# The opening of a Nyström-attention and two-layer kernel, emitted from a written list of single steps

## The chip, the cores and the metric

The kernel runs on one core of one Trainium2 chip. The metric is device time in microseconds (us) from the start to the end of the program on that core. The engines named below are PE (matmuls), DVE (vector), ACT (activations and copies), POOL (GpSimd), and SP, which here only issues DMA transfers. Each engine takes its instructions strictly in the order in which the program emits them, so the order of emission decides what an engine waits for.

## What is computed

A batch of 8 with 8 heads of 576 rows and 64 columns goes through a Nyström approximation of attention with 32 landmarks, and the result through two feed-forward blocks. Cut to what matters:

```python
q_lm, k_lm = mean of q and of k over each of 32 segments of 18 rows
A, Bm, C = softmax(q k_lm'), softmax(q_lm k_lm'), softmax(q_lm k')   # all scaled by 1/8
Z = Bm' / (norm1(Bm) * norminf(Bm) + 1e-6)
for _ in range(6): Z = 2 * Z - Z @ Bm @ Z
x = A @ Z @ C @ v                        # 4608 tokens, 512 wide
h = ((x @ w1) * (x @ w2)) @ w3           # 1024 wide, the gated block
x = h @ w_out1
g = elu(x @ w_in2)                       # 2048 wide
out = g @ w_out2
```

## The kernel before

**Stages.** The program has an opening, then 128 gated units, then 72 units of the second block. A gated unit is one batch, one half of its 576 rows and one eighth of the 1024 columns of the gated block. `ab(u)` makes its two products on PE (12 matmuls into two PSUM buffers), `ab_product(u)` copies one of them on ACT and multiplies on DVE, `ab_split(u)` splits the product into a high and a low part (ACT, then DVE), and `yy(u)` multiplies both with the folded weight and accumulates over eight units (12 matmuls).

**What the opening has to make.** (1) The weights arrive as 64-bit words and are rebuilt as float32, in 40 *conversions* of 128x512 in the opening (16 of w3, 8 of w_out1, 16 of w1 and w2 together). One conversion is: a load by SP, two ACT instructions (tiles `w_y` or `wo_y`, and `w_r` or `wo_r`), a short 16-bit DVE instruction on `w_y` or `wo_y`, a longer one into `cw` or `sw`, and an addition, on POOL for all but two conversions. Each of two pools has three buffers for what is loaded, so a load waits until an older conversion has been read. (2) w3 and w_out1 are folded into one weight by 16 *fold steps* on PE of four 128x512 matmuls (`w3o_step`, tile `w3acc`, 8 matmul records each in the trace). (3) The attention of batch 0, and most of that of batch 1: sums of q and k on DVE, scores `b`, `c` and `a` on PE, six Newton steps `n`, each a PE product and a DVE update of X, the transposes `ct`, the products `cv` and `z`, and the tiles `m` (`m_tiles`, one of four column groups each: eight matmuls, two copies `mh` on ACT, two differences `ml` on DVE). Unit 0 needs z, two `m` tiles and the rows `ath`/`atl` of `a`.

**Buffers that couple the steps.** All small attention products (`b`, `c`, `a`, `n`, `ct`, `cv`, `z`, `m`) share two PSUM buffers (`ps_at`, `bufs=2`): the next such product waits until ACT or DVE has read the one two before it. The pair of products of `ab` has two more (`ps_mm`).

**What sets the order.** Conversions are generators in `Pipe`, two at a time in the order of `ORDER`: each tick of the loop moves every running pair on by one stage and starts one new pair. After each tick the loop runs 1 or 2 half steps (`RATE = 1.6`) of the attention of batch 0, from the table that `Attention.steps` fills, and the half steps at which batch 1 is loaded and summed are given by `L1S`, `KS` and `QS`:

```python
while (i - A0) * RATE < NST or (1, NP - 1) not in w12_done or w3o_left:
    pipe.tick(len(pipe.todo) > n_late - HOLD)
    ...
    for hs in range(int((i - A0) * RATE), int((i - A0 + 1) * RATE)):
        run_steps(st0, hs)
```

Within a tick the four stages of a pair stand together on each engine: both `w_y`, both `w_r`, both long DVE instructions, both additions. The first two `m` tiles follow the loop. Then units start at u = 0 in the loop over `units`, whose `fill` runs half steps of the next batches, the last conversions of w1 and w2, and the conversions of the second block's weights (`pipe2`).

Of the kernel before, what the change touches and what calls it, by code (L numbers as in the profile page):

```python
# [24 lines left out]
NP = H // 2  # L25
# [22 lines left out]
QS = 20  # L48
RATE = 1.6
GAP = 2  # L50
CONV = (1, 5, 11, 14, 18)
M2 = 5
M3 = 10
VT = 7
W3B = 5
AH = 1
LT = 1
H_MAX = 4079.0


@with_exitstack
def nystrom_moe_kernel(ctx, tc, qT, kT, vm, vr, w12, w3T, w_out1, w_in2, w_out2, out):
# [60 lines left out]
    def high_parts(jobs):  # L123
# [3 lines left out]
        for c in jobs:  # L127
# [5 lines left out]
    def bits_job(jobs, ahead=2, late=1):  # L133

        for c in jobs:
            load_raw(c)
        for _ in range(ahead):  # L140
            yield
        for c in jobs:
            c.y, c.r = c.t("y", "cy", BF16), c.t("r", "ct", U32)
            act.activation(c.y, c.top.bitcast(BF16), AF.Abs, scale=2.0 ** -112)
        for c in jobs:
            act.mul(c.r, c.mid, 2.0 ** -13)
        high_parts(jobs)
        yield
        for c in jobs:
            if callable(c.x):  # L150
                c.x = c.x()
            (dve if c.on_dve else pool).tensor_tensor(c.x.bitcast(U32), c.b, c.r, op=ALU.add)
        for _ in range(late):
            yield
        for c in jobs:
            if c.done is not None:
                c.done()

    held, spills = set(), []

# [125 lines left out]
    def flush():  # L286
        while later:
            later.pop(0)()
# [334 lines left out]
    stp = start_ctx.enter_context(tc.tile_pool(name="start", bufs=1))  # L623

    with tc.manual_schedule():
        pipe = Pipe()
        wo_x, w3_x, acc = {}, {}, {}
        w3o_out = []
        w3o_left = {(ph, k) for ph in range(2) for k in range(K1)}

        def run_steps(st, i):
            for f, a in st.get(i, ()):
# [2 lines left out]
        def w3o_step(ph, k):  # L635
            if k == 0:
                acc[ph] = [ps_acc.tile([128, 512], F32, name=f"w3acc{ph}{j}", tag=f"acc{j}") for j in range(4)]
            for j in range(4):
                pe.matmul(acc[ph][j], w3_x[ph, k][:, j * 128 : (j + 1) * 128], wo_x[k], start=(k == 0), stop=(k == K1 - 1))
            w3o_left.remove((ph, k))  # L640
            if k == K1 - 1:
                for j in range(4):
                    o = (w3o_hi[4 * ph + j], w3o_lo[4 * ph + j], acc[ph][j])
                    if ph == 0:
                        split(*o)
                    else:
                        w3o_out.append(o)

        def wo_tile(k):
            wo_x[k] = stp.tile([128, DM], F32, name=f"wo{k}")  # L650
# [6 lines left out]
        w12_done = set()  # L657

        def w12_conv(p, jn, hp, on_dve):
            return Conv(  # L660
                p, f"w12{jn}{hp}", w12[hp, :, jn * 512 : (jn + 1) * 512], on_dve,
                x=w12_sb[:, hp, jn * 512 : (jn + 1) * 512], done=lambda: w12_done.add((jn, hp)),
            )

        def w3_conv(p, ph, k, on_dve):
            return Conv(
                p, f"w3{ph}{k}", w3T[k * 128 : (k + 1) * 128, ph * 512 : (ph + 1) * 512], on_dve,
                x=lambda: w3_tile(ph, k), done=lambda: w3o_step(ph, k),
            )

        w12_todo = [(jn, hp) for jn in range(4) for hp in range(NP)]
        w3_todo = [(ph, k) for ph in range(2) for k in range(K1)]

        def w12_next(p, on_dve):
            return w12_conv(p, *w12_todo.pop(0), on_dve)

        def w3_next(p, on_dve):
            return w3_conv(p, *w3_todo.pop(0), on_dve)

        n_wo = 0  # L680
        for o in ORDER:
            if o == "A":
                k, n_wo = n_wo, n_wo + 1
                wo = Conv(cvp, f"wo{k}", w_out1[k * 128 : (k + 1) * 128, :], False, x=lambda k=k: wo_tile(k))
                pair = [wo, w3_next(stp, k < E2)]
            elif o == "P":
                pair = [w3_next(cvp, False), w3_next(stp, False)]
            elif o == "B":
                pair = [w12_next(cvp, False), w3_next(stp, False)]
            elif o == "W":  # L690
                pair = [w12_next(cvp, False), w12_next(stp, False)]
            pipe.add(bits_job(pair, ahead=AH, late=LT))
        n_late = len(w12_todo)
        while w12_todo:
            pipe.add(bits_job([w12_next(cvp, False)]))

        make_words(cvp, "cw")
        make_words(stp, "sw")
        for w in PRE:
            if w != "-":  # L700
                load_in(0, w)
            pipe.tick()
        make_identity(nc, ident)
        for bd in (*qpad, cvbd):
            pool.memset(bd, 0.0)
# [6 lines left out]
        for hp in range(NP):  # L712
            st0[hp].extend(st0.pop((-16, -14, -12, -11)[hp]))
        L1 = dict(zip("kqv", L1S))
        S1 = {}
        for hp in range(NP):
            for w, o, hs in (("k", KS, (-16, -14, -12, -11)[hp]), ("q", QS, hp)):
                steps[1].pop(hs)
                S1.setdefault(o + hp, []).append((w, hp))
        i = 0  # L720
        while (i - A0) * RATE < NST or (1, NP - 1) not in w12_done or w3o_left:
            pipe.tick(len(pipe.todo) > n_late - HOLD)
            if i == VT:
                load_in(0, "v")
            for hs in range(int((i - A0) * RATE), int((i - A0 + 1) * RATE)):
                run_steps(st0, hs)
                for w in "kqv":
                    if hs == L1[w]:
                        load_in(1, w)
                for w, hp in S1.pop(hs, ()):  # L730
                    atts[1].sums(w, hp)
            i += 1
        for n, rest in enumerate(S1.values()):
            steps[1].setdefault(n, []).extend((atts[1].sums, wh) for wh in rest)
        start_ctx.close()
        mlp_ctx = ExitStack()
        mlp = mlp_ctx.enter_context(tc.tile_pool(name="mlp", bufs=1))

        units = [(b, n, fc) for b in range(B) for n in range(2) for fc in range(K1)]
        gt = {}  # L740
# [201 lines left out]
        def fill(b, hs):  # L942
            run_steps(steps[b + 1], hs)
            run_steps(steps[b], hs + 32)
            run_steps(steps[b + 2], hs - 32)
            if pipe.busy():
                pipe.tick()
            else:
                pipe2.tick(hs in CONV)
            if w3o_out:  # L950
                split(*w3o_out.pop(0))
            mt = [(atts[b + 1], m_next[hs])] if b + 1 < B and hs in m_next else []
            own = m_own if b else m_first
            if hs in own:
                while (own[hs], NP - 1) not in w12_done:
                    pipe.tick()
                mt.append((atts[b], own[hs]))
# [130 lines left out]
```

## Time and profile before

| | us |
|---|---|
| median of 3 runs | 1403.71 (1403.01 to 1405.25) |
| the profiled execution | 1403.01 |
| its span, first to last instruction | 1401.2 |
| first matmul of unit 0 | 105.1 |
| first matmul of unit 16 | 178.3 |
| PE busy, whole span | 1356.7 (97%) |

The page splits the span into 40 slices of 35 us. From the fifth slice on PE is busy at 9 tenths or more in each but the last; in the first four it stands at 6, 8, 7 and 8 tenths. The granted clock of PE reads 9 tenths or more in every slice but the third, where it reads 8. So the stretch to read is the first 180 us, by engine and by wait. A busy PE there includes matmul records stretched by a wait for their operands.

### The profile page before, as it was taken

Reading aid. Unit: us, or ns where it says so; the run is one execution under the profiler, and the core shown is the slowest. Engines: PE = TensorE matmul, PEld = TensorE weight load, DVE = VectorE, ACT = ScalarE, POOL = GpSimd, SP = SyncE. Lnnn points to the kernel's source line nnn. Section 1 sums busy time; section 2 is a strip of 40 time slices with the busy share of each in tenths; the row PEclk is TensorE's granted clock in tenths of the full one; section 3 lists DMA queues with packets and bytes.
Section 4 is the critical chain, followed back from the end, with each engine's and each line's share of the span. In section 5 each row is a group of like instructions: output and inputs, shape, how many; then the busy total and the mean of one; then the engine's idle time right before and its main releaser. Section 6 shows DMA issues by size and latency. Waiting matters only on the chain.

```text
span 1401.2 us, 26871 instructions
## 1 busy us (share of the span) xinstructions
PE 1356.7 (97%) x10848; PEld 1175.1 (84%) x10848; DVE 1031.0 (74%) x1830; ACT 628.3 (45%) x1263; POOL 332.5 (24%) x351
## 2 busy tenths in 40 slices
PE   6878999999999999999999999999999999999998
PEld 2326888988898889898899899899899899899897
DVE  6887867686668675635887878788687787878774
ACT  5535453545344444433353444344344453444342
POOL 5541425334345345112201011010100101011000
PEclk9989999999999999999999999999999999999999
DMA  9853454554474453246965564655655555564540
GB/s 339 276 175 129 153 174 155 200 191 135 158 260 142 157 183 128 101 157 254 367 221 189 208 220 159 229 199 188 207 196 214 176 223 189 206 223 158 196 150 31
DMA packets 59468, 266.76 MB, mean 190 GB/s; under 512 B 5584, under 2 KB 14800, under 8 KB 47056
## 3 DMA queue, kind: packets, MB, share of 16 engines
q0 software_dynamic: 12672, 140.51, 27.8%
q1 hardware_dynamic: 46672, 124.54, 25.6%
q8 instruction: 85, 1.39, 0.4%
q14 instruction: 39, 0.32, 0.1%
HBM read 223.08 MB, written 41.94 MB: 189 GB/s over the span
## 4 chain that ended last, share of the span: by engine, by line
PE 72%; DVE 2%; DMA 1%; ACT 0%; issue 0%; SPq 0%; ACTq 0%; DVEq 0%
PE o L919 9%; PE o L918 9%; PE o L917 9%; PE hm L858 9%; PE hm L859 8%; PE hm L860 8%; PE y L780 3%; PE ab L753 3%; PE y L782 2%; PE y L781 2%; PE ab L754 2%; PE ab L755 2%; PE m L331 1%; DMA w_raw<-in_w_in_dram 1%; PE n L615 0%; PE cv L387 0%
## 5 line engine op out<-in xcount | busy, mean ns | idle before, releaser
L858 PE MATMUL hm<-yb,wh 128*128 128x256 f32 x1008 | 285.2, 283 | 2.5 <-DVE g L876 1.7
L859 PE MATMUL hm<-yb,wh 128*128 128x256 f32 x1008 | 285.0, 283 | 0.0
L860 PE MATMUL hm<-yb,wh 128*128 128x256 f32 x1008 | 284.9, 283 | 0.0
L919 PE MATMUL o<-wo,el 128*128 128x512 f32 x576 | 225.6, 392 | 0.0
L918 PE MATMUL o<-wo,eh 128*128 128x512 f32 x576 | 225.3, 391 | 0.0
L917 PE MATMUL o<-wo,eh 128*128 128x512 f32 x576 | 224.0, 389 | 0.0
L889 ACT ACTIVATE t<-m 128x512 f32<-128x512 f32 x144 | 89.9, 624 | 297.9 <-DVE m L887 297.9
L858 PEld LDWEIGHTS hm<-yb,wh 128*128 128x128 f32 x1008 | 192.9, 191 | 5.6 <-DVE g L876 1.9
L859 PEld LDWEIGHTS hm<-yb,wh 128*128 128x128 f32 x1008 | 192.9, 191 | 2.8
L860 PEld LDWEIGHTS hm<-yb,wh 128*128 128x128 f32 x1008 | 193.0, 191 | 0.0
L804 POOL DMA_DIRECT2D wh<-wh_d x72 | 39.6, 550 | 611.4 <-PE hm L860 606.9
L780 PE MATMUL y<-gh,w3oh 128*128 128x288 f32 x512 | 159.8, 312 | 1.8 <-DVE w3ol L68 1.8
L892 DVE SCALAR_TENSOR_TENSOR t<-m,t 128x512 f32<-128x512 f32 x144 | 99.1, 688 | 77.9 <-ACT m L890 77.9
L753 PE MATMUL ab<-ath,mh 128*128 128x288 f32 x512 | 156.0, 305 | 0.2 <-ACT a L762 0.2
L782 PE MATMUL y<-gh,w3ol 128*128 128x288 f32 x512 | 151.6, 296 | 0.0
L781 PE MATMUL y<-gl,w3oh 128*128 128x288 f32 x512 | 151.4, 296 | 0.0
L754 PE MATMUL ab<-atl,mh 128*128 128x288 f32 x512 | 151.3, 296 | 0.0
L755 PE MATMUL ab<-ath,ml 128*128 128x288 f32 x512 | 150.8, 294 | 0.0
L764 DVE TENSOR_TENSOR g<-ab,a 128x288 f32<-128x288 f32 x128 | 58.1, 454 | 103.2 <-ACT gh L67 60.5
L780 PEld LDWEIGHTS y<-gh,w3oh 128*128 128x128 f32 x512 | 96.6, 189 | 38.1 <-issue 23.2
L919 PEld LDWEIGHTS o<-wo,el 128*128 128x128 f32 x576 | 108.1, 188 | 22.7
L917 PEld LDWEIGHTS o<-wo,eh 128*128 128x128 f32 x576 | 108.5, 188 | 20.9
(141 smaller groups left out, 2669.3 us busy)
## 6 DMA issues: line engine op xcount, KB each, us to landing
wh<-wh_d POOLq DMA_DIRECT2D x72, 1792.0 KB, 7.8
wo_raw<-in_w_out_dram SPq DMA_DIRECT2D x24, 512.0 KB, 5.3
k<-in_kT_dram SPq DMA_DIRECT2D x8, 1152.0 KB, 7.1
q<-in_qT_dram SPq DMA_DIRECT2D x8, 1152.0 KB, 5.1
yd<-ysb SPq DMA_DIRECT2D x16, 576.0 KB, 3.7
yin<-yd SPq DMA_DIRECT2D x9, 1024.0 KB, 10.0
out_dram<-osb SPq DMA_DIRECT2D x36, 256.0 KB, 2.3
w_raw<-in_w3T_dram SPq DMA_DIRECT2D x16, 512.0 KB, 6.9
```

What stands on the lines that cost most here:

```text
L753: pe.matmul(p[:, :NH], mh[:, cs], ah[:, blk, :], start=(blk == 0), stop=False)
L754: pe.matmul(p[:, :NH], mh[:, cs], al[:, blk, :], start=False, stop=False)
L755: pe.matmul(p[:, :NH], ml[:, cs], ah[:, blk, :], start=False, stop=(blk == 1))
L780: pe.matmul(a[oc][:, :NH], w3o_hi[fc][:, os_], gh, start=(fc == 0), stop=False)
L781: pe.matmul(a[oc][:, :NH], w3o_hi[fc][:, os_], gl, start=False, stop=False)
L782: pe.matmul(a[oc][:, :NH], w3o_lo[fc][:, os_], gh, start=False, stop=(fc == K1 - 1))
L858: pe.matmul(o, ah, bh[:, kk, :], start=(kk == 0), stop=False)
L859: pe.matmul(o, ah, bl[:, kk, :], start=False, stop=False)
L860: pe.matmul(o, al, bh[:, kk, :], start=False, stop=(kk == 1))
L917: pe.matmul(a, eh[:, ts_], w[:, 0, :], start=first, stop=False)
L918: pe.matmul(a, eh[:, ts_], w[:, 1, :], start=False, stop=False)
L919: pe.matmul(a, el[:, ts_], w[:, 0, :], start=False, stop=last)
```

## The change

The loops of the opening, the half steps of batch 0 in it and the first 16 passes of the loop over units are replaced by a string of 486 words, `OPENING`, that is read from left to right. Each word is one step: `L5`, `y5`, `r5`, `h5`, `w5`, `x5`, `o5` are the seven stages of conversion 5 (load, the two ACT instructions, the two DVE instructions, the addition, and the fold step that it makes possible), `:0a1` is the second `a` score of batch 0, `:1n3` a Newton step of batch 1, `:0m0` an `m` tile, `:0l` the `ml` differences that stand out, `s4` to `s7` the split of the second half of the folded weight (`s0` to `s3` the first), `A3 G3 D3 Y3` are `ab`, `ab_product`, `ab_split` and `yy` of unit 3, `P0` and `P1` a tick of `pipe2`. Conversions no longer run in pairs, and no rate ties their stages to the steps of the attention. The loop over units begins at u = 16.

```diff
-A0 = 1
-L1S = (12, 19, 20)
-PRE = "-k-q"
-HOLD = 1
-NST = 24
-KS = 15
-QS = 20
-RATE = 1.6
...
+OPENING = """
+L1 L0 L3 y1 id r1 L6 L7 y0 L2 h1 w1 y3 r0 L5 r3 x1 h0 h3 w0 w3 r7 x3 L4 y7 y6 h6 r6 y5 x0 y2 o1 r2 h7 w6 L15
+y4 w7 :0iq h5 y15 h2 h4 L8 w5 w2 x6 r5 x2 :0ik h15 x7 :0q0 L9 r15 y8 :0q1 L11 r4 :0q3 :0q2 w15 x5 w4 r8 o3 h8
...
-        a0, st0 = atts[0], steps[0]
...
-        i = 0
-        while (i - A0) * RATE < NST or (1, NP - 1) not in w12_done or w3o_left:
-            pipe.tick(len(pipe.todo) > n_late - HOLD)
-            if i == VT:
-                load_in(0, "v")
-            for hs in range(int((i - A0) * RATE), int((i - A0 + 1) * RATE)):
-                run_steps(st0, hs)
...
+        def do(t):
+            if t[0] == ":":
+                attention_step(atts[int(t[1])], t[2:])
+            elif t[0] in CONV_STEPS:
+                CONV_STEPS[t[0]](convs[int(t[1:])])
+            elif t[0] == "s":
+                w3o_split(*divmod(int(t[1:]), 4))
+            elif t[0] == "P":
+                pipe2.tick(t[1] == "1")
...
+            else:
+                {"A": ab, "G": ab_product, "D": ab_split, "Y": yy}[t[0]](int(t[1:]))
...
-        for jn in range(2):
-            a0.m_tiles(jn)
-            flush()
-        m_own, m_next, m_first = {0: 2, 2: 3}, {24: 0, 28: 1}, {M2: 2, M3: 3}
+        m_own, m_next = {0: 2, 2: 3}, {24: 0, 28: 1}
+
+        for t in OPENING.split():
+            do(t)
...
-        for u in range(nu + LAG):
+        for u in range(2 * K1, nu + LAG):
```

Every instruction of before is still there, once, with the same shape. Up to the first matmul of unit 16 each queue holds as many instructions as before: 781 rows on PE, 174 on ACT, 74 on POOL, 71 on SP, and on DVE 270 where there were 268.

**SP, the first loads of the program.** A name such as `w301_raw` is the load for fold step 1 of the first half, `wo1_raw` the block of w_out1 that goes with it; `k0` and `q0` are batch 0. Before:

```order
L119 DMA wo0_raw_118<-in_w_out1_dram 128x2048
L119 DMA w300_raw_120<-in_w3T_dram 128x2048
L280 DMA k0_122<-in_kT_dram 128x2304
L119 DMA wo1_raw_136<-in_w_out1_dram 128x2048
L119 DMA w301_raw_138<-in_w3T_dram 128x2048
L119 DMA wo2_raw_156<-in_w_out1_dram 128x2048
L119 DMA w302_raw_158<-in_w3T_dram 128x2048
L280 DMA q0_160<-in_qT_dram 128x2304
```

and now:

```order
L126 DMA w300_raw_118<-in_w3T_dram 128x2048
L126 DMA wo0_raw_120<-in_w_out1_dram 128x2048
L126 DMA w301_raw_122<-in_w3T_dram 128x2048
L126 DMA wo3_raw_135<-in_w_out1_dram 128x2048
L126 DMA w303_raw_137<-in_w3T_dram 128x2048
L126 DMA wo1_raw_141<-in_w_out1_dram 128x2048
L126 DMA w302_raw_149<-in_w3T_dram 128x2048
L126 DMA wo2_raw_163<-in_w_out1_dram 128x2048
L126 DMA w307_raw_190<-in_w3T_dram 128x2048
L261 DMA q0_195<-in_qT_dram 128x2304
L126 DMA wo4_raw_202<-in_w_out1_dram 128x2048
L261 DMA k0_212<-in_kT_dram 128x2304
```

q and k went behind nine and ten loads of weights, and the block `wo1` of the second fold step from fourth to sixth.

**PE, after the second `a` score of batch 0.** Before, `cv` follows it at once:

```order
L331 MATMUL a_0_734<-q_160,ksum_247 32x288
L331 MATMUL a_0_735<-q_160,ksum_247 32x288
L387 MATMUL cv_749<-v_470,ct_582 32x64 x20
L639 MATMUL w3acc_439<-wo_346,w_712 128x512
L639 MATMUL w3acc_440<-wo_346,w_712 128x512
```

and now a fold step does, and a Newton product after it:

```order
L312 MATMUL a_0_587<-q_195,ksum_243 32x288
L312 MATMUL a_0_588<-q_195,ksum_243 32x288
L618 MATMUL w3acc_513<-wo_272,w_542 128x512
L618 MATMUL w3acc_514<-wo_272,w_542 128x512
L618 MATMUL w3acc_515<-wo_272,w_542 128x512
L618 MATMUL w3acc_516<-wo_272,w_542 128x512
L596 MATMUL n_0_617<-X_532 32x64 x8
```

The product that needs the PSUM buffer of `a` now stands behind four matmuls that need none.

**PE, from `cv` to the `m` tiles of batch 0.** Before:

```order
L387 MATMUL cv_749<-v_470,ct_582 32x64 x20
L639 MATMUL w3acc_439<-wo_346,w_712 128x512
L639 MATMUL w3acc_440<-wo_346,w_712 128x512
L639 MATMUL w3acc_441<-wo_346,w_712 128x512
L639 MATMUL w3acc_442<-wo_346,w_712 128x512
L387 MATMUL cv_749<-v_470,ct_582 32x64 x20
L406 MATMUL z_830<-X_688,cvbd 64x32 x8
L331 MATMUL m_0_861<-w_sb,z_839 32x512
L331 MATMUL m_0_862<-w_sb,z_839 32x512
```

and now:

```order
L368 MATMUL cv_738<-v_673,ct_479 32x64 x20
L618 MATMUL w3acc_513<-wo_403,w_709 128x512
L618 MATMUL w3acc_514<-wo_403,w_709 128x512
L618 MATMUL w3acc_515<-wo_403,w_709 128x512
L618 MATMUL w3acc_516<-wo_403,w_709 128x512
L387 MATMUL z_824<-X_774,cvbd 64x32 x8
L618 MATMUL w3acc_513<-wo_384,w_808 128x512
L618 MATMUL w3acc_514<-wo_384,w_808 128x512
L618 MATMUL w3acc_515<-wo_384,w_808 128x512
L618 MATMUL w3acc_516<-wo_384,w_808 128x512
L312 MATMUL m_0_871<-w_sb,z_833 32x512
L312 MATMUL m_0_872<-w_sb,z_833 32x512
```

A fold step now stands between `cv` and `z` and another between `z` and the first `m` tile. The two `m` tiles and unit 0 follow each other as before.

## Rows read from the trace of the kernel before

**Rows 1.** Windows: stretch, then busy us (and instructions) of PE, PEld, DVE, ACT, POOL; PE's granted clock, DMA share, GB/s.
```profile
0.00:10.40 10.40, 0.00 (x1) 0.03 (x1) 3.35 (x5) 3.70 (x5) 3.65 (x9) 1.00 0.83 296
10.40:58.70 48.30, 44.99 (x170) 17.88 (x170) 42.20 (x75) 30.72 (x57) 28.65 (x24) 1.00 0.92 330
58.70:105.10 46.40, 33.72 (x288) 14.01 (x288) 35.82 (x67) 19.15 (x34) 20.59 (x15) 0.80 0.56 186
105.10:135.00 29.90, 23.69 (x208) 19.18 (x201) 22.22 (x50) 18.54 (x42) 6.41 (x5) 0.92 0.39 126
135.00:178.30 43.30, 43.30 (x523) 37.58 (x523) 33.92 (x72) 17.79 (x40) 18.16 (x18) 1.00 0.48 156
```
**Rows 2.** Waits of PE up to unit 16: in total, times, longest.
```profile
PE w3acc L639 <- DVE w L152: 10.4, 1, 10.4
PE m L331 <- DVE ml L419: 4.2, 1, 4.2
PE cv L387 <- DVE at L428: 3.9, 1, 3.9
PE a L331 <- DVE X L617: 3.6, 1, 3.6
PE bs L548 <- DVE ml L419: 2.2, 1, 2.2
PE ct L369 <- DVE ml L419: 2.2, 1, 2.2
PE m L331 <- DVE z L411: 1.9, 1, 1.9
PE w3acc L639 <- POOL w L152: 1.8, 4, 0.7
PE y L780 <- DVE w3ol L68: 1.8, 1, 1.8
```
**Rows 3.** Timeline of PE: start, us, instruction; in brackets the idle time before it.
```profile
10.40 9.33 PE L639 MATMUL w3acc<-wo,w 128*128 128x512 f32 x16 [10.40 <-DVE w L152]
...
45.21 7.13 PE L639 MATMUL w3acc<-wo,w 128*128 128x512 f32 x16
...
62.08 5.45 PE L639 MATMUL w3acc<-wo,w 128*128 128x512 f32 x8
...
105.12 0.61 PE L753 MATMUL ab<-ath,mh 128*128 128x288 f32 x1
...
178.30 0.30 PE L753 MATMUL ab<-ath,mh 128*128 128x288 f32 x1
```
**Rows 4.** Timeline of DVE: the first conversion, and the stretch around the second `a` score.
```profile
5.19 0.29 DVE L126 TENSOR_SCALAR wo_y<-wo_y 128x512 uint16<-128x512 uint16 x1 [5.19 <-ACT wo_y L144]
...
79.65 2.24 DVE L126 TENSOR_SCALAR w_y<-w_y 128x512 uint16<-128x512 uint16 x2
81.81 1.80 DVE L129 SCALAR_TENSOR_TENSOR cw<-w_raw,w_y 128x512 uint16<-128x512 uint16 x1
...
85.45 0.83 DVE L428 STREAM_TRANSPOSE at<-a 128x288 f32<-128x288 f32 x2
```
**Rows 5.** Timeline of POOL in the same stretch.
```profile
80.42 1.31 POOL L152 TENSOR_TENSOR w_sb<-cw,w_r 128x512 uint32<-128x512 uint32 x1
81.70 1.32 POOL L152 TENSOR_TENSOR w<-sw,w_r 128x512 uint32<-128x512 uint32 x1
```
**Rows 6.** Groups of DVE by line up to unit 16: busy us, mean ns of one, idle before.
```profile
L126 DVE TENSOR_SCALAR w_y<-w_y 128x512 uint16<-128x512 uint16 x34 | 15.6, 475 | 6.0 <-ACT w_y L144 6.0
...
L126 DVE TENSOR_SCALAR wo_y<-wo_y 128x512 uint16<-128x512 uint16 x9 | 6.1, 682 | 8.0 <-ACT wo_y L144 7.9
```
**Rows 7.** Windows again, columns as in the first group: a stretch with DMA full.
```profile
10.00:15.00 5.00, 4.60 (x6) 2.04 (x7) 2.71 (x6) 3.38 (x6) 1.18 (x1) 1.00 1.05 428
```
**Rows 8.** The page's DMA issues: KB each, us from issue to landing.
```profile
q<-in_qT_dram SPq DMA_DIRECT2D x8, 1152.0 KB, 5.1
...
w_raw<-in_w3T_dram SPq DMA_DIRECT2D x16, 512.0 KB, 6.9
```

More of the change, by code (lines that the diff above doesn't have):

```diff
@@ L131, in high_parts @@
             )
[L133 to L157, printed above, removed]
     held, spills = set(), []
@@ L625, in nystrom_moe_kernel @@
     with tc.manual_schedule():
-        pipe = Pipe()
+        pipe2 = Pipe()
         wo_x, w3_x, acc = {}, {}, {}
-        w3o_out = []
-        w3o_left = {(ph, k) for ph in range(2) for k in range(K1)}
         def run_steps(st, i):
@@ L639, in w3o_step, with w3o_split @@
                 pe.matmul(acc[ph][j], w3_x[ph, k][:, j * 128 : (j + 1) * 128], wo_x[k], start=(k == 0), stop=(k == K1 - 1))
[L640 to L647, printed above, removed]
+        def w3o_split(ph, j):
+            split(w3o_hi[4 * ph + j], w3o_lo[4 * ph + j], acc[ph][j])
         def wo_tile(k):
@@ L655, in w3_tile, with w12_conv, w3_conv @@
             return w3_x[ph, k]
-        w12_done = set()
-        def w12_conv(p, jn, hp, on_dve):
+        def w12_conv(p, jn, hp):
             return Conv(
-                p, f"w12{jn}{hp}", w12[hp, :, jn * 512 : (jn + 1) * 512], on_dve,
-                x=w12_sb[:, hp, jn * 512 : (jn + 1) * 512], done=lambda: w12_done.add((jn, hp)),
+                p, f"w12{jn}{hp}", w12[hp, :, jn * 512 : (jn + 1) * 512],
+                x=w12_sb[:, hp, jn * 512 : (jn + 1) * 512],
             )
-        def w3_conv(p, ph, k, on_dve):
+        def w3_conv(p, ph, k):
@@ L666, in w3_conv, with wo_conv @@
             return Conv(
-                p, f"w3{ph}{k}", w3T[k * 128 : (k + 1) * 128, ph * 512 : (ph + 1) * 512], on_dve,
+                p, f"w3{ph}{k}", w3T[k * 128 : (k + 1) * 128, ph * 512 : (ph + 1) * 512], ph == 0 and k < E2,
                 x=lambda: w3_tile(ph, k), done=lambda: w3o_step(ph, k),
             )
+        def wo_conv(k):
+            return Conv(cvp, f"wo{k}", w_out1[k * 128 : (k + 1) * 128, :], x=lambda: wo_tile(k))
         w12_todo = [(jn, hp) for jn in range(4) for hp in range(NP)]
@@ L672, in nystrom_moe_kernel @@
         w3_todo = [(ph, k) for ph in range(2) for k in range(K1)]
[L674 to L680, printed above, removed]
+        convs = []
         for o in ORDER:
             if o == "A":
-                k, n_wo = n_wo, n_wo + 1
-                wo = Conv(cvp, f"wo{k}", w_out1[k * 128 : (k + 1) * 128, :], False, x=lambda k=k: wo_tile(k))
-                pair = [wo, w3_next(stp, k < E2)]
+                convs += [wo_conv(len(convs) // 2), w3_conv(stp, *w3_todo.pop(0))]
@@ L686, in nystrom_moe_kernel @@
             elif o == "P":
-                pair = [w3_next(cvp, False), w3_next(stp, False)]
+                convs += [w3_conv(cvp, *w3_todo.pop(0)), w3_conv(stp, *w3_todo.pop(0))]
             elif o == "B":
[L689 to L705, printed above, removed]
+                convs += [w12_conv(cvp, *w12_todo.pop(0)), w3_conv(stp, *w3_todo.pop(0))]
+            else:
+                convs += [w12_conv(cvp, *w12_todo.pop(0)), w12_conv(stp, *w12_todo.pop(0))]
+        convs += [w12_conv(cvp, *t) for t in w12_todo]
@@ new lines, in conv_y, with conv_r, conv_h, conv_w @@
+        def conv_y(c):
+            c.y = c.t("y", "cy", BF16)
+            act.activation(c.y, c.top.bitcast(BF16), AF.Abs, scale=2.0 ** -112)
+        def conv_r(c):
+            c.r = c.t("r", "ct", U32)
+            act.mul(c.r, c.mid, 2.0 ** -13)
+        def conv_h(c):
+            c.m = c.y.bitcast(U16)
+            dve.tensor_scalar(c.m, c.m, H_MAX, 8.0, op0=ALU.min, op1=ALU.mult)
+        def conv_w(c):
+            c.b = words(c)
+            dve.scalar_tensor_tensor(
+                c.b.bitcast(U16)[:, 1:1024:2], c.top, 0x8000, c.m, op0=ALU.bitwise_and, op1=ALU.bitwise_or
+            )
@@ L707, in nystrom_moe_kernel, with conv_x @@
+        def conv_x(c):
+            if callable(c.x):
+                c.x = c.x()
+            (dve if c.on_dve else pool).tensor_tensor(c.x.bitcast(U32), c.b, c.r, op=ALU.add)
+        CONV_STEPS = {"L": load_raw, "y": conv_y, "r": conv_r, "h": conv_h, "w": conv_w, "x": conv_x, "o": lambda c: c.done()}
         atts = [Attention(b) for b in range(B)]
@@ L733, in nystrom_moe_kernel, with attention_step @@
-        for n, rest in enumerate(S1.values()):
-            steps[1].setdefault(n, []).extend((atts[1].sums, wh) for wh in rest)
-        start_ctx.close()
-        mlp_ctx = ExitStack()
-        mlp = mlp_ctx.enter_context(tc.tile_pool(name="mlp", bufs=1))
+        def attention_step(a, what):
+            lm, n = a.lm, int(what[-1]) if what[-1].isdigit() else None
+            {
+                "k": lambda: a.sums("k", n), "q": lambda: a.sums("q", n), "p": lambda: lm.q_pad(n),
+                "b": lm.b_scores, "be": lm.b_exp, "bs": lm.b_soft, "bn": lm.b_norms, "bx": lm.b_norms2,
+                "r": lm.r0, "n": lambda: lm.newton(n), "c": lambda: a.c_scores(n), "cm": lambda: a.c_max(n),
+                "ce": lambda: a.c_exp(n), "cn": a.c_norm, "t": lambda: a.c_trans(n), "v": lambda: a.cv(n), "z": a.zcv,
+                "a": lambda: a.a_scores(n), "am": a.a_max, "as": a.a_sub, "ae": a.a_exp, "au": a.a_sum,
+                "af": lambda: a.a_mul(n), "ah": lambda: a.a_split(n), "m": lambda: a.m_tiles(n), "l": flush,
+                "L": lambda: a.slice_load("kq"[n // NP], n % NP), "S": lambda: a.slice_sum("kq"[n // NP], n % NP),
+                "ik": lambda: load_in(a.b, "k"), "iq": lambda: load_in(a.b, "q"), "iv": lambda: load_in(a.b, "v"),
+            }[what.rstrip("0123456789")]()
@@ new lines, in nystrom_moe_kernel, with opened @@
+        make_words(cvp, "cw")
+        make_words(stp, "sw")
+        mlp_ctx = ExitStack()
+        mlp = None
+        def opened():
+            nonlocal mlp
+            start_ctx.close()
+            mlp = mlp_ctx.enter_context(tc.tile_pool(name="mlp", bufs=1))
+        def do(t):
[7 more added lines that the diff above has]
+                pipe2.tick(t[1] == "1")
+            elif t == "=":
+                opened()
+            elif t == "id":
+                make_identity(nc, ident)
+                for bd in (*qpad, cvbd):
+                    pool.memset(bd, 0.0)
+            else:
+                {"A": ab, "G": ab_product, "D": ab_split, "Y": yy}[t[0]](int(t[1:]))
@@ L945, in fill @@
             run_steps(steps[b + 2], hs - 32)
[L946 to L951, printed above, removed]
-            mt = [(atts[b + 1], m_next[hs])] if b + 1 < B and hs in m_next else []
[L953 to L957, printed above, removed]
+            pipe2.tick(hs in CONV)
+            mt = [(atts[b + 1], m_next[hs])] if b + 1 < B and hs in m_next else []
+            if hs in m_own:
+                mt.append((atts[b], m_own[hs]))
             for a, jn in mt:
                 a.m_tiles(jn)
-        for u in range(nu + LAG):
+        for u in range(2 * K1, nu + LAG):
             if u < nu:
```

37 lines of the change are left out of this document (17 added, 20 removed).

## The prediction

> **What bounds the kernel now.** First the timeline of PE gives the two marks between which the change lies: unit 0 starts at 105.1 us and unit 16 at 178.3 [rows 3]. Each queue holds the same instructions ahead of unit 16 as before (two small DVE ones apart), and the emission from there on is the same. So the 1401.2 - 178.3 = 1222.9 us behind that mark stay, and only the mark can move. Second, the windows up to it [rows 1]: PE is never idle from 135 to 178.3, while ahead of 135 it loses time in every window, and its granted clock falls to a mean of 0.80 and 0.92 in two of them. Third, the waits of PE [rows 2]: beside the 10.4 us until the first matmul, eight lines make 21.6 us of idle time, and nearly all name DVE. Fourth, DVE's busy time in the same windows: 3.35 + 42.20 + 35.82 = 81.4 us ahead of unit 0, and 22.22 + 33.92 = 56.1 us from there to unit 16. DVE is thus occupied for 81.4 of the first 105.1 us; an order of emission can't push unit 0 ahead of what DVE has to do for it, unless the instructions get shorter.
>
> **What PE loses before, in all.** (1) The first 10.4 us. (2) The two first fold steps take 9.33 us where two take 7.13 later [rows 3]: 2.2 us. (3) 21.6 us of waits. (4) The low clock: a mean of 0.80 over 46.4 us is 18.6 us at 1.2 instead of 2.4 GHz, and PE was busy 33.72 of 46.4 us there, so about 13.5 busy us at half speed, which is 6.7 us lost; in the same way 0.92 over 29.9 us with 23.69 busy gives 1.9. In sum 42.8, of which 32.4 come after the first matmul. A PE without any of these would reach unit 16 at 178.3 - 32.4 = 146 us. That is the floor on this side.
>
> **Part 1, up to unit 0.** The chain through PE gets much shorter. The `a` wait of 3.6 goes: its product now comes as soon as two fold steps are done, ahead of the Newton chain. The `cv` wait of 3.9 goes: PE waited there for the buffers of `a`, whose transposes on DVE stood behind two `w_y`, `cw` and more [rows 4]; now a fold step (7.13 / 2 = 3.6 us) lies between. The wait of `m` for z (1.9) goes under the last fold step. Newton products alternate with fold steps, and the DVE work between two updates of X lies beside these. One wait stays: the second `m` tile follows the first directly, and needs `mh` and `ml` of the first to be made. Before it cost 4.2 us, with other DVE work ahead of `ml`; at its nearest kin, the `bs` and `ct` waits for `ml`, 2.2 [rows 2]. I take 2.2, with 4.2 as the other end.
>
> With that PE would reach unit 0 at 105.1 less 15.4 of waits (4.2, 3.9, 3.6, 1.9, 1.8), less 6.7 of clock, less 2.2, plus 2.2, that is 83. But DVE can't: its 81.4 busy us and the 7.0 us that it is idle in the first 10.4 make 88.4 [rows 1]. The first 7.0 stay, because the first load and the first addition come no earlier. Of the 48.3 - 42.2 = 6.1 idle us of the second window I keep 4: they are waits for loads early on. The second fold step now needs the sixth load instead of the fifth, and k stands behind ten weight loads and q: 10 x 512 + 2 x 1152 KB are 7.6 MB, of which 3.1 are moved by 10.4 us (at 296 GB/s) and the rest at 428 GB/s by 21 [rows 1, 7, 8]. That is well ahead of the fold steps that are to cover the rest of the chain. Of the 46.4 - 35.8 = 10.6 of the third window I keep 3, around the `m` tiles; the rest were waits for PE products that now have conversion work in front of them. So unit 0 starts at 81.4 + 7.0 + 4 + 3 = 95.4: **9.7 us earlier**, with DVE as the later side.
>
> **What DVE's own length may do.** The short 16-bit step takes 0.29 us when alone [rows 4], but 43 of them took 15.6 + 6.1 = 21.7 us [rows 6], where 43 x 0.29 = 12.5: 9.2 us over. The stretched ones lie beside additions on POOL: two took 2.24 us while POOL ran additions of 1.31 and 1.32 [rows 4, 5]. The list changes which pairs meet, and the trace of before can't show how. I bound it by none (-9.2) and twice as many (+9.2) and take as many as before. The Trainium skill ("SBUF — State Buffer", section "SBUF: two separate sides") says that DVE and GpSimd take a shared pair of ports as an exclusive lock for a whole instruction and the loser waits fully. By that rule all 43 could be blocked for an addition each; the trace has a mean of 0.2 us each.
>
> **Part 2, units 0 to 15.** It took 73.2 us. PE lost there 1.8 + 2.2 + 2.2 of waits [rows 2] and 1.9 of clock, in sum 8.1. The two `ml` waits go, since the two later `m` tiles are now followed by products of units, not by one that needs their buffers. The 1.8 is the wait of the first `yy` for the split of the folded weight, which is now spread ahead of it. Against that, units 4 and 5, 6 and 7, and 13 and 14 now stand back to back in the two PSUM buffers of `ab`, and each pair waits for a copy and a product of the unit before: I put 0.8 us on each, in all 2.5, an estimate from the 2.2 that a pair of copy and difference cost above. DVE has 56.1 us of work in the stretch and so keeps up. The part takes 73.2 - 8.1 + 2.5 = 67.6: **5.6 us less**.
>
> **Sum.** 9.7 + 5.6 = 15.3 us off the profiled execution's 1403.0 gives 1387.7. The median of the runs lies 0.7 above that execution, so the time is 1388.4; I say 1388.
>
> **Rivals.** *More comes off (1375 to 1382).* If additions and 16-bit steps meet half as often and DVE's idle time shrinks to that of the start, unit 0 comes at about 87; with part 2 that is 24 us, 1380. At the end of it both the clock's and DVE's losses vanish and unit 16 starts at 148: 30 us, 1374. For it: nothing of PE's chain stands against it. Against: DVE and PE would both be busy almost without a break, in fixed orders that wait on each other.
>
> *Less comes off (1394 to 1400).* The stretched steps are twice as many: 9.2 us back on DVE ahead of unit 0, and some 6 are left, 1398. For it: the list puts the additions of one conversion directly beside the 16-bit steps of the next.
>
> *Nothing.* DVE is so full that any order gives the same: within 0.2%, that is 2.8 us, which is about what a measurement of this kernel can tell from no change. Against: 23.7 of its 105.1 us were idle.
>
> *Slower: the clock stays low while PE works in pieces.* In the opening PE now pauses ahead of the second fold step and the first `c`. Before, the clock came down after pauses of 3.6 and 3.9 us (mean of 0.80 around them [rows 1]), and a fold step then took up to 5.45 us [rows 3]. If it stayed down through the eight fold steps of the first half, each would take 2 x 3.6 us: 8 x 3.6 = 28 us more, which passes the 15 gained from the fifth such step on, 1416. Against: before, each fall was over within a few fold steps, and PE is full again behind the first `c`. The Trainium skill ("TensorE: Matmul & The Clock Gate", section "HAM oscillation — how this bites in real kernels") describes this very case, a kernel whose waits for loads make each block of matmuls start at the low clock. The trace shows single falls, not one at each step.
>
> **How the numbers follow.** The forecast (1382 to 1394) has 0.51, more 0.19, beyond even that 0.02, less 0.13, nothing 0.05, slower 0.10. Faster by over 0.2% is the first four: 0.85. The range takes in the forecast, more and less, 1374 to 1400, with 0.83. Its ends are the bounds above: 30 us off where DVE's stretching and every removable loss go, 4 off where the stretching doubles and the `m` wait stays 4.2.
>
> **What would show it.** Right: unit 0 starts at 91 to 99 and unit 16 at 159 to 167; PE's waits on `a`, `cv` and z are gone from its list, one on `ml` of about 2 stays; the span behind unit 16 is again 1223. DVE's busy time ahead of unit 0 is again 81, and that is the number I trust least: 72 speaks for the first rival, 90 for the second. A granted clock well below 0.80 in the first 60 us speaks for the last. Wrong altogether would be a stretch behind unit 16 that is longer than before, or DVE idle for 20 us ahead of unit 0.

## The result, and the profile after

The changed kernel takes **1380.24 us** (median of 4 runs, 1378.98 to 1382.18) where the kernel before, on the same chip, takes 1404.26 (1403.01 to 1405.25): a ratio of 0.9831, with a 95% interval of 0.9814 to 0.9848. That is 24.0 us off; the forecast was 15.3 off. The profiled execution took 1379.11 us, with a span of 1377.3.

The timeline of PE after the change (start, us, instruction; in brackets the idle time before it and what ended it) gives the marks that [rows 3] gives for before:

```profile
11.86 5.30 PE L618 MATMUL w3acc<-wo,w 128*128 128x512 f32 x8 [11.86 <-POOL wo L681]
19.07 3.70 PE L618 MATMUL w3acc<-wo,w 128*128 128x512 f32 x8 [1.91 <-POOL wo L681]
...
87.82 1.68 PE L312 MATMUL m<-w_sb,z 64*32 64x512 f32 x16 [1.51 <-DVE ml L400]
89.43 0.40 PE L745 MATMUL ab<-ath,mh 128*128 128x288 f32 x1
...
153.11 0.29 PE L745 MATMUL ab<-ath,mh 128*128 128x288 f32 x1
```

Unit 0 starts at 89.4 us (before 105.1) and unit 16 at 153.1 (before 178.3): 15.7 us come off ahead of unit 0, and 9.5 more between the two marks, which are 63.7 us apart and not 73.2. Behind unit 16 lie 1224.2 us where there were 1222.9: 1.3 us are given back, in a part that issues the same instructions in the same order. One stretch at the low clock falls in it; the profile of before has none there:

```profile
315.50:318.90 3.40, 3.40 (x43) 3.23 (x32) 1.32 (x5) 1.48 (x4) 0.00 (x0) 0.50 0.59 235
```

The columns are those of the next windows; 0.50 is the clock. The kernels below and the repeated profiles bear out that this is what was given back: the six profiles without such a fall have 1221.7 to 1223.6 us behind unit 16, the six with one 1224.2 to 1225.4, the two with two 1225.5 and 1225.9.

The windows (stretch, then busy us and instructions of PE, PEld, DVE, ACT, POOL; granted clock, DMA share, GB/s), cut at unit 0 and unit 16, answer to [rows 1]:

```profile
0.00:11.90 11.90, 0.04 (x1) 0.04 (x1) 4.52 (x8) 5.69 (x9) 5.05 (x14) 1.00 0.81 290
11.90:58.70 46.80, 42.72 (x196) 17.75 (x196) 40.42 (x88) 32.20 (x60) 25.37 (x19) 0.96 0.86 309
58.70:89.43 30.73, 29.22 (x278) 12.76 (x262) 27.12 (x56) 17.61 (x31) 17.83 (x13) 1.00 0.76 271
89.43:153.11 63.68, 63.68 (x729) 54.65 (x723) 53.13 (x121) 34.46 (x78) 27.46 (x25) 1.00 0.56 186
```

Three things are to be seen. PE is busy for all of the last window: no wait is left between the two marks. The granted clock, 0.80 and 0.92 in two windows of before, is 0.96 to 1.00. And DVE's busy time ahead of unit 0 is 4.52 + 40.42 + 27.12 = 72.1 us, where before it was 81.4, for nearly the same instructions. PE's waits up to unit 16, all of them (in total, times, longest), are these; [rows 2] has nine lines, in sum 32.0 us:

```profile
PE w3acc L618 <- POOL wo L681: 13.8, 2, 11.9
PE m L312 <- DVE ml L400: 1.5, 1, 1.5
PE c L312 <- ACT e L323: 1.5, 1, 1.5
PE c L312 <- DVE wo_y L670: 0.7, 1, 0.7
```

Where DVE's 9.3 us went is read from its groups by line up to unit 16 (busy us, mean ns of one, idle before), which answer to [rows 6]:

```profile
L670 DVE TENSOR_SCALAR w_y<-w_y 128x512 uint16<-128x512 uint16 x32 | 11.6, 376 | 8.4 <-ACT w_y L662 8.3
L670 DVE TENSOR_SCALAR wo_y<-wo_y 128x512 uint16<-128x512 uint16 x8 | 2.2, 289 | 1.3 <-ACT wo_y L662 1.3
```

The short 16-bit step has become shorter: 376 and 289 ns where it took 475 and 682 (three of the 43 stand at another line now, L133, at 278 and 289). Ahead of unit 0, 36 of them take 13.0 us, where 35 took 19.1. The timelines of DVE and of POOL show why some are long. DVE:

```profile
13.13 0.29 DVE L670 TENSOR_SCALAR w_y<-w_y 128x512 uint16<-128x512 uint16 x1
...
14.58 1.35 DVE L670 TENSOR_SCALAR w_y<-w_y 128x512 uint16<-128x512 uint16 x1
...
81.51 1.08 DVE L670 TENSOR_SCALAR w_y<-w_y 128x512 uint16<-128x512 uint16 x1
```

and POOL:

```profile
14.21 1.58 POOL L681 TENSOR_TENSOR wo<-cw,wo_r 128x512 uint32<-128x512 uint32 x1 [2.40 <-DVE cw L674]
...
81.19 1.26 POOL L681 TENSOR_TENSOR w_sb<-sw,w_r 128x512 uint32<-128x512 uint32 x1
```

A short step that begins while POOL is in the middle of an instruction ends only about 0.15 us after that one's end (15.93 after 15.78, 82.60 after 82.45); the step that begins at 13.13, while POOL stands still, takes 0.29. Counted over both timelines up to unit 0, 12 of 35 short steps began under a POOL instruction before, and took 12.5 us together; now 7 of 36 do, and take 4.7. The other 23 and 29 took 6.6 and 8.3, none of them over 0.35.

### The profile page after: what moved, and what is told of

Read it like the earlier page. It is cut to its first block, busy times and chain, and to the rows that moved or that the text cites. A ratio compares the mean times of both kernels' runs of the same rounds, so it can differ in the third digit from the quotient of the medians.

```text
span 1377.3 us, 26846 instructions
## 1 busy us (share of the span) xinstructions
PE 1349.0 (98%) x10848; PEld 1173.5 (85%) x10848; DVE 1019.4 (74%) x1830; ACT 628.4 (46%) x1263; POOL 330.7 (24%) x351
## 4 chain that ended last, share of the span: by engine, by line
PE 73%; DVE 2%; DMA 1%; ACT 0%; issue 0%; SPq 0%; ACTq 0%; DVEq 0%
PE o L909 10%; PE o L910 10%; PE o L908 9%; PE hm L849 9%; PE hm L850 9%; PE hm L851 9%; PE y L772 3%; PE ab L745 3%; PE y L774 3%; PE y L773 3%; PE ab L746 3%; PE ab L747 2%; PE m L312 1%; DMA w_raw<-in_w_in_dram 1%; PE n L596 1%; PE cv L368 0%
## 5 line engine op out<-in xcount | busy, mean ns | idle before, releaser
L908 PEld LDWEIGHTS o<-wo,eh 128*128 128x128 f32 x576 | 108.5, 188 | 20.9
L909 PEld LDWEIGHTS o<-wo,eh 128*128 128x128 f32 x576 | 108.1, 188 | 21.2
```

The lines of the kernel that those rows point to most:

```text
L908: pe.matmul(a, eh[:, ts_], w[:, 0, :], start=first, stop=False)
L909: pe.matmul(a, eh[:, ts_], w[:, 1, :], start=False, stop=False)
```

## The experiments

Unless said otherwise every kernel here computes the same thing as before, in another order of emission. Times are medians of runs beside runs of the kernel before on the same chip, ratios are to that one. The marks, from the timelines and windows of one profiled execution each (us):

| kernel | unit 0 | units 0 to 15 | DVE busy / idle ahead of unit 0 | median | ratio |
|---|---|---|---|---|---|
| before | 105.1 | 73.2 | 81.4 / 23.7 | 1404.26 | 1 |
| after | 89.4 | 63.7 | 72.1 / 17.4 | 1380.24 | 0.9831 (0.9814 to 0.9848) |
| old order to unit 0, then new | 105.5 | 71.6 | 81.4 / 24.1 | 1401.72 | 0.9982 (0.9973 to 0.9992) |
| new order to unit 0, then old | 90.1 | 78.3 | 72.5 / 17.6 | 1393.03 | 0.9930 (0.9909 to 0.9951) |
| after, conversions in pairs | 93.6 | 65.8 | 79.7 / 13.9 | 1384.72 | 0.9859 (0.9844 to 0.9874) |
| before, conversions in the new order | 114.6 | 75.0 | 81.1 / 33.5 | 1411.72 | 1.0042 (1.0028 to 1.0055) |
| after, short step twice | 101.4 | 64.8 | 87.3 / 14.1 | 1391.36 | 0.9907 (0.9893 to 0.9922) |
| before, short step twice | 114.1 | 77.5 | 92.8 / 21.3 | 1418.67 | 1.0108 (1.0094 to 1.0122) |
| after, short step ahead of its long one | 92.1 | 64.4 | 80.1 / 12.0 | 1383.44 | 0.9860 (0.9846 to 0.9873) |

**The two parts, each alone.** The first kernel has the order of before up to unit 0 and then that of the changed one; the second the reverse:

```diff
-L1 L0 L3 y1 id r1 L6 L7 y0 L2 h1 w1 y3 r0 L5 r3 x1 h0 h3 w0 w3 ...
+L0 L1 :0ik y0 y1 r0 r1 h0 h1 w0 w1 L2 L3 x0 x1 y2 y3 r2 r3 h2 h3 w2 w3 ...
```

> The order of before up to unit 0, written as words, and the order of the changed kernel for all that is left then. If the two parts of the gain are separate (15.7 us ahead of unit 0, 9.5 us from there to unit 16 in the two traces): unit 0 at 105, unit 16 at 105 + 64 = 169, total near 1395. If the gain behind unit 0 was only work that the new opening had done earlier or a clock that it had kept up, part two takes 73 as before and the total is 1403 to 1404.

```diff
-... A0 w32 L36 w35 :0l G0 :1b A1 s7 y39 s6 h39 G1 s5 :1c0 D0 L38 :0af1 ...
+... :0l w32 x32 A0 G0 :1iv :0l :0l L36 s5 A1 G1 :0l D0 :0af1 w35 L37 s6 ...
```

> The reverse: the order of the changed kernel up to unit 0, and that of before for what is left. If the parts are separate: unit 0 at 89 to 90, unit 16 at 162 to 163, total near 1389. If the units' gain comes from the opening, unit 16 at 153 and 1380.

Neither forecast of either kernel holds. The new opening alone gives 15.0 of the 15.7 us at unit 0. But the two parts don't add up: the units' new order behind the old opening takes 1.6 us less, the old one behind the new opening 5.1 us more, and both new 9.5 us less. Two windows (columns as above), of the units in the first kernel and in the second:

```profile
105.50:177.10 71.60, 68.04 (x729) 57.31 (x723) 54.65 (x123) 36.08 (x82) 24.71 (x23) 0.94 0.47 153
```

```profile
90.10:168.40 78.30, 67.95 (x729) 57.45 (x723) 56.86 (x119) 34.74 (x78) 27.46 (x25) 0.96 0.42 138
```

In the first PE is idle for 3.6 us, and its clock is below full; in the second it is idle for 10.4, and the waits of PE there are mainly these:

```profile
PE bs L530 <- DVE ml L401: 4.7, 1, 4.7
PE y L773 <- DVE w3ol L76: 3.0, 2, 1.7
PE ct L351 <- DVE ml L401: 2.2, 1, 2.2
```

These are the waits for `ml` and for the split of the folded weight that [rows 2] shows. The units' new order takes them away: the first kernel has none of them, but its largest wait is one that the changed kernel doesn't have, for a step on the scores `b`:

```profile
PE c L312 <- DVE bm L538: 3.1, 1, 3.1
```

So what the new order puts in their place isn't all there in time behind the old opening.

**Conversions back in pairs, or unpaired alone.** Into the slots that conversion steps have in the changed list, their old paired order is put; and the reverse, into the old slots the new order (ahead of each of the first three fold steps five to seven conversion steps are drawn forward, since it needs what they make; from the third on 17 more stand ahead of each fold step than before).

```diff
-L1 L0 L3 y1 id r1 L6 L7 y0 L2 h1 w1 y3 r0 L5 r3 x1 h0 h3 w0 w3 ...
+L0 L1 y0 y1 id r0 r1 h0 h1 w0 w1 ...
```

> The fold steps, the attention and the units in the new order, and the 206 words of the conversions put into the same places in the order of before: two at a time, both short DVE steps together, both additions together. Theory one (DVE is the later side ahead of unit 0, and its instructions got 9.3 us shorter because short steps and additions on POOL meet less): the stretched steps return, DVE is busy for about 81 us ahead of unit 0, unit 0 at 96 to 99, total 1386 to 1390. Theory two (what counts is where the fold steps stand on PE; DVE's length was by the way): unit 0 at 89 to 91, total 1380 to 1382.

> The order of the kernel before, in which the 240 conversion words alone (loads, ScalarE, VectorE and GpSimd steps) stand in the order of the changed kernel, in the old slots; fold steps, attention steps and units keep their old places. Theory one (conversions no longer in pairs and the new places of the other steps add up; with the pairs put back into the changed kernel unit 0 came 4.2 us later): unit 0 at 100 to 102, VectorE's busy time up to it 74 to 77, median 1397 to 1401. Rival (the old places of fold and attention steps set the opening by themselves, whatever VectorE has to do): VectorE's busy time falls, unit 0 stays within 1.5 us of 105.1, median 1402 to 1405.

Pairs put back, the result lies between the two theories: the short steps take 19.3 us again and DVE's busy time is 79.7, but unit 0 comes only 4.2 us later. Ahead of unit 0, 10 of 36 short steps begin under a POOL instruction. The groups of DVE up to 115 us:

```profile
L670 DVE TENSOR_SCALAR w_y<-w_y 128x512 uint16<-128x512 uint16 x32 | 15.2, 484 | 2.6 <-ACT w_y L662 2.6
L670 DVE TENSOR_SCALAR wo_y<-wo_y 128x512 uint16<-128x512 uint16 x8 | 5.1, 638 | 5.6 <-ACT wo_y L662 5.6
```

So 11.5 of the 15.7 us ahead of unit 0 are there with paired conversions too: the new places of the fold and attention steps, and of the slots between them, give them by themselves. Which of these moves gives how much wasn't tried. The reverse kernel let both of its theories fall: it is slower than before, unit 0 at 114.6. Its waits of PE and, below, of DVE:

```profile
PE w3acc L619 <- POOL wo L682: 16.8, 3, 14.1
PE m L313 <- DVE z L393: 5.5, 1, 5.5
PE cv L369 <- DVE at L410: 3.6, 1, 3.6
```

```profile
DVE w_y L671 <- ACT w_y L663: 14.3, 6, 6.0
```

PE starts 3.7 us later, and 12 of 38 short steps begin under a POOL instruction. The 14.3 us are not what is new: in the kernel before DVE's two lines of waits for `wo_y` and `w_y` make 13.9 [rows 6], so the 9.8 us by which DVE is idle longer lie in waits that it doesn't have, the longest of them 2.8 us for the load of q. The new order of the conversions brings no fewer meetings with POOL in itself; they became fewer only together with the steps that the changed list puts between them. Which of the moved loads and slots costs most wasn't tried.

**Is DVE the side that sets unit 0?** The short step is done twice; the added one is a minimum with the same bound and a product with one, which changes no value.

```diff
+            dve.tensor_scalar(c.m, c.m, H_MAX, 1.0, op0=ALU.min, op1=ALU.mult)
             dve.tensor_scalar(c.m, c.m, H_MAX, 8.0, op0=ALU.min, op1=ALU.mult)
```

On the new order:

> The changed kernel with one more short 16-bit step in each of the 40 conversions of the opening, the same minimum taken once more, which changes no value. Ahead of unit 0 that is some 37 x 0.2 to 0.29 = 7 to 11 us of DVE. Theory one: unit 0 comes 7 to 11 us later (97 to 100), total 1387 to 1391. Theory two: DVE is idle for 17.4 us ahead of unit 0 and takes it: unit 0 at most 2 us later, total 1380 to 1383.

On the old one:

> The order of the kernel before, with each conversion's short 16-bit step done twice (a minimum and a multiplication by one come on top, and change no value). Theory one (VectorE sets the start of unit 0 under the old order too): the 10 to 15 us that come on top of its 81.4 us move unit 0 by 0.8 of that, as under the new order (12.0 for 15.2): from 105.1 to 113 to 117, the median 1412 to 1417. Rival (under the old order the waits between the engines set the opening, and VectorE's 23.7 us without work take the added steps): unit 0 moves by 4 us at most, the median is 1404 to 1408.5.

DVE's windows up to unit 0, of the new order and of the old one:

```profile
0.00:101.40 101.40, 77.86 (x458) 32.23 (x458) 87.35 (x186) 55.60 (x99) 48.68 (x47) 0.94 0.75 260
```

```profile
0.00:114.10 114.10, 79.07 (x458) 32.37 (x458) 92.82 (x181) 54.00 (x95) 53.75 (x48) 0.90 0.70 243
```

15.2 us more of DVE put unit 0 off by 12.0, and under the old order 11.4 more put it off by 9.0: as the first theories had it in kind, though on the new order by more (11 of the 72 short steps begin under a POOL instruction now), and with a median 1.7 us above the forecast on the old one. So 0.8 us per us of DVE in both, although DVE under the old order has 23.7 us without work: little of that time is a reserve. That it lies in chains where DVE waits for ACT or PE and they for it is a reading: the added step also stands in each conversion's own way to PE, and work on DVE outside those ways wasn't added.

**Where the short step stands.** In the changed list, often the short steps of two or three conversions come first and then their long ones. Here each stands directly ahead of its own long one (not quite as in the kernel before, where the two short steps of a pair come ahead of its two long ones):

```diff
-... x1 h0 h3 w0 w3 r7 x3 L4 y7 y6 h6 r6 y5 x0 y2 o1 r2 h7 w6 ...
+... x1 h0 w0 h3 w3 r7 x3 L4 y7 y6 r6 y5 x0 y2 o1 r2 h6 w6 ...
```

> The changed kernel with one kind of step moved: each conversion's short 16-bit VectorE step is put directly ahead of its long one, as in the kernel before; every other step keeps its place. Theory one (the short step's place against GpSimd's additions sets its length, and VectorE sets unit 0): the 36 short steps ahead of unit 0 go from 13.0 us toward the 19.1 to 19.3 us of the paired orders, VectorE's busy time there from 72 to 76 or more, unit 0 from 89.4 to 92 to 94, the median 1382.5 to 1385. Rival (it is the places of the additions themselves, which stay): the short steps take 13 to 14 us, unit 0 stays within 1 us of 89.4, the median 1379 to 1381.5.

The time and unit 0 (92.1) came as the first theory had it, and DVE's busy time rose by 8.0, but not by the carrier that I named: the short steps take 12.3 us, even less than in the changed kernel. It is the long ones that grew, as the groups of DVE up to 90 us show; in the changed kernel these two take 12.3 us, 734 ns and 6.3 us, 798 ns:

```profile
L674 DVE SCALAR_TENSOR_TENSOR sw<-w_raw,w_y 128x512 uint16<-128x512 uint16 x17 | 15.7, 924 | 1.3
L674 DVE SCALAR_TENSOR_TENSOR cw<-wo_raw,wo_y 128x512 uint16<-128x512 uint16 x8 | 9.0, 1126 | 0.4
```

One place in the timelines of DVE and POOL tells how:

```profile
38.41 0.75 DVE L674 SCALAR_TENSOR_TENSOR sw<-w_raw,w_y 128x512 uint16<-128x512 uint16 x1
39.04 0.29 DVE L670 TENSOR_SCALAR wo_y<-wo_y 128x512 uint16<-128x512 uint16 x1
39.36 1.84 DVE L674 SCALAR_TENSOR_TENSOR cw<-wo_raw,wo_y 128x512 uint16<-128x512 uint16 x1
```

```profile
39.33 1.27 POOL L681 TENSOR_TENSOR w<-sw,w_r 128x512 uint32<-128x512 uint32 x1 [1.83 <-DVE wo_y L670]
```

The addition adds what the long step at 38.41 made, and begins 0.17 us after that one's end, just as the short step between them ends; the next long step, which needs the short one's output, starts 0.03 us later and lasts until 41.20, 0.6 us after the addition. Seven of 35 long steps did this, 12.4 us in all, where the changed kernel has two.

**Versions meant to be faster.** PE waits 1.91 us in the changed kernel for the second block of w_out1. The first version has that block two places earlier (conversions 2 and 6 exchanged), w0 ahead of h3, and r0 ahead of y3:

```diff
-L1 L0 L3 y1 id r1 L6 L7 y0 L2 h1 w1 y3 r0 L5 r3 x1 h0 h3 w0 w3 ...
+L1 L0 L3 y1 id r1 L2 L7 y0 L6 h1 w1 r0 y3 L5 r3 x1 h0 w0 h3 w3 ...
```

> The changed kernel, with the start of its list mended where its trace shows TensorE waiting for the second block of the output weights: conversions 2 and 6 exchange places, so that the second fold step's block is rebuilt by 15.8 us and not by 19.0; and conversion 0's second ScalarE step and long VectorE step stand one place earlier. Theory one (VectorE alone sets unit 0): TensorE starts some 0.6 us earlier and its wait of 1.91 us goes, and unit 0 stays within 1 us of 89.4, median 1379 to 1381. Rival (what TensorE loses at the start counts in full): unit 0 at 86.5 to 87.5, median 1377 to 1378.5.

> As the kernel with conversions 2 and 6 exchanged, and the fold step of conversion 7 moved ahead of the first attention product, into the gaps of 0.7 and 1.5 us that TensorE has there. Theory one (VectorE alone sets unit 0): the attention's products come 1 to 3 us later, which delays what VectorE does on them; unit 0 at 89 to 92, median 1379.5 to 1382.5. Rival (TensorE's gaps count): unit 0 at 85 to 87, median 1375.5 to 1378.

The second version also has the fold step `o7` ahead of the first `c` product. Medians of 1381.08 (0.9841, 0.9827 to 0.9854) and 1380.82 (0.9839, 0.9824 to 0.9854), unit 0 at 90.8 and 91.2. PE's first matmul comes 1.1 us earlier in both, and unit 0 later by 1.4 and 1.8: what PE wins at the start doesn't arrive there. The first version misses both of its forecasts for unit 0, the second meets its first theory. In the first the gain is lost at the first `c` product already, which waits for DVE and comes at 23.50 us, where the changed kernel has it at 23.49 after a wait of 0.7:

```profile
23.50 0.72 PE L312 MATMUL c<-k,qsum 64*32 64x288 f32 x16 [3.90 <-DVE wo_y L670]
```

The timelines of DVE and POOL in that version:

```profile
8.51 0.74 DVE L674 SCALAR_TENSOR_TENSOR cw<-wo_raw,wo_y 128x512 uint16<-128x512 uint16 x1
9.14 0.28 DVE L670 TENSOR_SCALAR w_y<-w_y 128x512 uint16<-128x512 uint16 x1
9.51 1.75 DVE L674 SCALAR_TENSOR_TENSOR sw<-w_raw,w_y 128x512 uint16<-128x512 uint16 x1
```

```profile
9.40 1.26 POOL L681 TENSOR_TENSOR wo<-cw,wo_r 128x512 uint32<-128x512 uint32 x1 [5.28 <-DVE cw L674]
```

With `h3` between `w0` and `w3`, the addition that `w0` releases begins first, and `w3` takes 1.75 us; in the changed list w0 and w3 stand together. So a third version exchanges conversions 2 and 6 alone, and moves one short step (`h33`) behind `:0z`:

```diff
-:1q3 h33 y32 o27 :3L2 x34 :0z r33 ...
+:1q3 y32 o27 :3L2 x34 :0z h33 r33 ...
```

> The changed kernel, conversions 2 and 6 exchanged (the second fold step's output-weight block earlier) but conversions 0 and 3 left as they are, since there the long step that was moved behind its neighbour's began under a running GpSimd addition and took 1.75 us; and one short step (conversion 33, 1.08 us under an addition) behind the product it delayed. Theory (each addition that a conversion step no longer meets is worth a part of a microsecond at unit 0, the earlier block 1 us): unit 0 at 87.5 to 89, median 1378.5 to 1380. Rival (VectorE's order has slack there): unit 0 at 89 to 90.5, median 1380 to 1381.5.

> The changed kernel as it is, beside the kernel with conversions 2 and 6 exchanged and conversion 33's short step moved, on the same chip: unit 0 at 89 to 90, median 1379 to 1381.

> The kernel with conversions 2 and 6 exchanged and conversion 33's short step moved, once more, on the same chip as the changed kernel. If the 1 us that its unit 0 gained is the move's: unit 0 0.5 to 1.5 us ahead of the changed kernel's and the median 1 to 2.5 us below it. Rival (the difference of 2.4 us between the two medians was that of two chips or of the clock's falls behind unit 16): the medians within 1 us.

It took 1377.83 us (0.9813, 0.9793 to 0.9833), and beside the changed kernel on one chip 1379.82 (1378.20 to 1381.65) against 1380.23 (1378.54 to 1382.22). Unit 0 is 0.9 us earlier in both of its profiles (88.5), but the medians on one chip differ by 0.4, less than the runs of either spread, as the rival had it: not shown to be faster.

## Why the prediction was right, and where it was off

**The direction and the place were right, the size was not.** 1380.24 us lies in the stated range, but not in the forecast's own 1382 to 1394: it is a time of the first rival, which had a chance of 0.19. Unit 0 at 89.4 and unit 16 at 153.1 are both ahead of the 91 to 99 and 159 to 167 that I named as signs of being right, by terms that are taken up below (6.0 us in part 1, 3.9 in part 2). And one sign of being wrong altogether came, a longer stretch behind unit 16: 1.3 us, which go with the one fall of the clock there. Time came off ahead of unit 0 and between units 0 and 16, and nearly none elsewhere. The waits of `a`, `cv` and z are gone from PE's list, as the first part had it, and one on `ml` stays, 1.5 us where I took 2.2. The fold steps do cover the chain, and DVE is the later side (0.8 us of unit 0 for each us of added short steps). With pairs put back, where DVE's work is 79.7 us and so near the 81.4 that I reckoned with, unit 0 comes at 93.6 against my 95.4: its DVE is idle for 7.0, 2.9 and 4.0 us in the three windows (cut at 12 and 58.7 us) where I had 7.0, 4 and 3, and the `ml` wait is 2.2. For a DVE of unchanged length the sum was right.

**The size of part 1 was off by one term.** The sum was 81.4 busy and 14.0 idle, 95.4; it is 72.1 and 17.4, 89.4. The stretching of the short steps I took as before, with -9.2 as the lower end, and DVE's busy time is 9.3 lower. That end wasn't a bound: the 9.2 were those of all 43 short steps up to unit 16, and other DVE steps had been stretched too. Two thirds of the 9.3 are the short steps (19.1 to 13.0 us); the rest is spread over small groups, such as one 128x2 step that had taken 1.21 us under an addition and now takes 0.15. The rule of the Trainium skill that I weighed there ("SBUF — State Buffer", section "SBUF: two separate sides") I set aside because the mean of all 43 was small. The timelines bear the rule out step by step: over before, after and the three kernels that move conversions, 45 of the 47 short steps that began under a POOL instruction were stretched (the other two began in its last 0.04 us), and none of the 133 that didn't. What I should have counted was how many begin under one, 12 of 35, which the trace of before held; how many would meet one under the new list it could not show. The idle time came out 3.4 above my 14.0 (7.4, 6.4 and 3.6 us in the three windows): with a shorter DVE other engines hold it up for longer, and the two kernels in which DVE is longer again (paired, and short step twice) have 13.9 and 14.1.

**Not all of the 9.3 counted.** With pairs put back, DVE has 7.6 us more to do and unit 0 comes 4.2 later; with each short step ahead of its long one it is 8.0 and 2.7. Its idle time takes the difference (17.4 to 13.9 and 12.0). So the first rival came true in the one half: 12 meetings became 7, and unit 0 is nearer to its 87 than to my 95. The other half, that DVE's idle time would shrink to that of the start, did not come.

**Part 2** was put at 67.6 us and took 63.7. The 2.5 us that I put on units standing back to back aren't there: PE has no wait in the stretch. The other 1.4: PE's busy time there fell by 3.3 us for the same work, where I had counted 1.9 for the clock. PE was busy in all of the 4.9 us at the low clock there, which makes 2.4; the last 0.9 no run explains. The two stretches in the kernel before:

```profile
105.12:106.58 1.46, 1.46 (x13) 1.46 (x7) 0.67 (x2) 1.07 (x2) 0.00 (x0) 0.50 0.07 24
120.25:123.66 3.41, 3.41 (x23) 3.08 (x28) 2.44 (x7) 0.26 (x1) 1.31 (x2) 0.50 0.00 0
```

**The clock** fell once ahead of unit 16 in the profile of the changed kernel, from 25.4 to 28.8 us, in the last of PE's three waits of 1.9, 0.7 and 1.5, and not at all up to unit 16 in a second profile. Before, it fell four times. The kernel with short steps done twice, in which PE waits 3.2 and 2.5 us, has four falls ahead of unit 16 again. The rival by which the clock would stay down did not come.

## What to carry to other kernels

Where two engines hold each other up, count in the timelines how many steps of the one begin while the other is at work, and how long those take: the mean over all of them hides a price that falls on few. An engine's idle time in such an opening is only in part a reserve: before calling it free, lengthen its work and see how much of that arrives at the end (here 0.3 to 0.8 of it). An order written out step by step is one object: of four kernels put together from parts of the two orders none came up to the changed kernel, and one was slower than both.

## What the runs showed of the chip

The long conversion step, 0.73 us, is held up by a POOL addition too (1.69 to 1.84 us, seven of 35 where it stands directly behind its short step), while the sums of q and k, which read one tile, are not: 9 of 16 began under an addition in the kernel before, and none took over 0.76, where those that met none took up to 0.75. Two long steps directly behind each other escape, since the addition that the first one releases begins only when the second is under way: x0 at 10.27 us, behind w3 at 10.00, in the changed kernel. The Trainium skill, in the section named above, counts DVE steps with two inputs in SBUF among those that wait for a GpSimd instruction that reads SBUF; the rows agree, with the addition winning wherever it starts first. In the kernel before, two long steps began under memsets on POOL (16.52 and 17.14 us), which read nothing, and took 0.72 us.
